# Storing the last group of an output pair by pair and moving the last subtraction from GpSimd to VectorE

## The chip, the cores and the metric

The kernel runs on one core of a Trainium2 chip. The metric is the device time of one execution in microseconds. Engines are named as in the profile: PE is TensorE (PEld its weight loads), DVE VectorE, ACT ScalarE, POOL GpSimd, SP SyncE. A "q" behind an engine's name means its sequencer.

## The reference

```
qn = q / (norm(q, axis=1) + 1e-6);  kn likewise          # q, k, v: 4 x 6336 x 256, f32
a  = softmax(kn^T @ qn / tau)                            # 256 x 256 for each batch
x  = (v @ a) as rows, 25344 x 256
H  = max(x @ w_h, 0);   T = sigmoid(x @ w_t + b_t)
out = T * H + (1 - T) * x
```

## The kernel before

A batch has 49 full slices of 128 rows and one of 64. They are worked on in 25 pairs per batch, 100 in all. For each pair PE makes z, h and x in PSUM, ACT the sigmoid tt, DVE two products th and ux, and POOL their difference. Four pairs share one output tile and go out as one store of 1 MB (1024 KB). The last pair of a batch is irregular: 128 rows and 64 rows, so two pieces and two stores. All loads but that of b_t (1 KB, by SP) cast f32 to f16 and are issued by POOL: 20 each for q and k, 12 for v, 3 for the remainders, 2 for the weights, 57 in all by the profile's list of DMA issues.

```python
    def store(t, ot):
        b, i = divmod(t, NPAIR)              # NPAIR = 25, OG = 4
        ob = out[b * N : (b + 1) * N]
        if i == NPAIR - 1:
            nc.sync.dma_start(out=rows(ob)[:, NS - 1 : NS, :], in_=ot[:, 0:1, :])
            nc.sync.dma_start(out=ob[NF:N, :], in_=ot[0:REM, 1, :])
        elif i % OG == OG - 1:
            s0 = 2 * (i - OG + 1)
            nc.sync.dma_start(out=rows(ob)[:, s0 : s0 + 2 * OG, :], in_=ot)

    def elementwise_ops(t, z, h, x, ps):
        ...                                  # tt = sigmoid(z); th = max(h,0)*tt; ux = (tt-1)*x
        ot, o0 = out_tile(t)
        for pr, us in parts:                 # one part; two in the last pair of a batch
            nc.gpsimd.tensor_tensor(
                out=ot[pr, o0 + us.start : o0 + us.stop, :], in0=th[pr, us, :],
                in1=ux[pr, us, :], op=AluOp.subtract,
            )
        store(t, ot)
```

## Time and profile before

| | before |
|---|---|
| time, median of the first 3 runs | 298.07 us (297.93 to 298.23) |
| span of the profiled run | 294.71 us |
| PE's last matmul ends | 287.13 us |
| POOL's last operation ends | 289.17 us |
| SP has seen the last store land and is through | 292.85 us |
| POOL's closing drain ends | 293.92 us |

At the end of the kernel every engine drains and meets the others at a barrier. The prediction below shows the lines. (It has 293.95 for the lowest row, from a start that its view rounds to 288.1; the trace has 288.06 + 5.86 = 293.92.)

One line is added that it doesn't show. It is from the list of PE's instructions at the end (start, duration, line, operation), and the end of that group, 287.13, is the zero: **tail** means from the end of PE's last matmul to the end of the span, here 294.71 - 287.13 = 7.58 us.

```profile
286.40 0.73 PE L366 MATMUL x<-mr,vts 128*128 128x256 f16 x4
```

The second line added is the page's group for PE's first matmul of the attention phase. Its last field is PE's idle time before it, 14.3 us, spent waiting for loads of k.

```profile
L185 PE MATMUL S<-q,k 128*128 128x256 f16 x392 | 88.0, 278 | 14.3 <-DMA k<-in_k_dram 14.3
```

### The profile page before, as it was taken

Reading aid. Unit: us, or ns where it says so; the run is one execution under the profiler, and the core shown is the slowest. Engines: PE = TensorE matmul, PEld = TensorE weight load, DVE = VectorE, ACT = ScalarE, POOL = GpSimd, SP = SyncE. Lnnn points to the kernel's source line nnn. Section 1 sums busy time; section 2 is a strip of 40 time slices with the busy share of each in tenths; the row PEclk is TensorE's granted clock in tenths of the full one; section 3 lists DMA queues with packets and bytes.
Section 4 is the critical chain, followed back from the end, with each engine's and each line's share of the span. In section 5 each row is a group of like instructions: output and inputs, shape, how many; then the busy total and the mean of one; then the engine's idle time right before and its main releaser. Section 6 shows DMA issues by size and latency. Waiting matters only on the chain.

```text
span 294.7 us, 6910 instructions
## 1 busy us (share of the span) xinstructions
PE 262.0 (89%) x2844; PEld 228.7 (78%) x2844; DVE 169.5 (58%) x318; ACT 163.5 (55%) x302; POOL 166.4 (56%) x175
## 2 busy tenths in 40 slices
PE   0497966999999999999999899999999888999990
PEld 0386944899999987899999786999998655999970
DVE  1000022675655585666666756556658777999990
ACT  1000035864453588565555596545557976989860
POOL 7111340596555775466665945455457545888882
PEclk9999988999999999999999999999999979999997
DMA  6999999999999999999999999999996631245434
GB/s 116 214 212 213 203 214 221 211 215 287 281 252 243 285 233 268 266 240 284 254 259 269 280 258 244 275 232 276 255 278 161 199 145 64 107 197 211 169 142 169
DMA packets 13233, 65.58 MB, mean 223 GB/s; under 512 B 1425, under 2 KB 3474, under 8 KB 8594
## 3 DMA queue, kind: packets, MB, share of 16 engines
q0 software_dynamic: 8848, 39.19, 65.8%
q1 hardware_dynamic: 4354, 25.96, 21.9%
q8 instruction: 22, 0.36, 0.4%
q14 instruction: 9, 0.07, 0.1%
HBM read 78.38 MB, written 25.95 MB: 354 GB/s over the span
## 4 chain that ended last, share of the span: by engine, by line
PE 72%; DMA 9%; ACT 6%; POOL 5%; DVE 4%; issue 2%; POOLq 0%; DVEq 0%
PE zbank L366 13%; PE x L366 13%; PE h L366 13%; PE S L185 11%; DMA k<-in_k_dram 9%; PE vtps L343 7%; PE G L188 6%; PE G L191 6%; POOL o L419 2%; DVE th L408 1%; PE ah L286 1%; DVE ux L413 1%; ACT tt L396 1%; ACT dcat L225 1%; PE cq L233 1%
## 5 line engine op out<-in xcount | busy, mean ns | idle before, releaser
L419 POOL TENSOR_TENSOR o<-th,ux 128x512 f32<-128x512 f32 x96 | 124.2, 1296 | 92.6 <-DVE ux L413 78.8
L366 PEld LDWEIGHTS <-vts 128*128 128x128 f16 x1200 | 109.7, 98 | 19.3 <-issue 7.9
L185 PE MATMUL S<-q,k 128*128 128x256 f16 x392 | 88.0, 278 | 14.3 <-DMA k<-in_k_dram 14.3
L396 ACT ACTIVATE tt<-zbank 128x512 f32<-128x512 f32 x100 | 59.6, 596 | 67.6 <-PE zbank L366 66.7
L408 DVE SCALAR_TENSOR_TENSOR th<-h,tt 128x512 f32<-128x512 f32 (+1 forms) x104 | 68.9, 666 | 48.6 <-PE h L366 28.4
L188 PE MATMUL G<-k 128*128 128x128 f16 x392 | 77.0, 223 | 0.0
L413 DVE SCALAR_TENSOR_TENSOR ux<-tt,x 128x512 f32<-128x512 f32 (+1 forms) x104 | 67.9, 656 | 0.7 <-PE x L366 0.7
L366 PE MATMUL x<-mr,vts 128*128 128x256 f16 (+1 forms) x400 | 61.1, 275 | 3.4 <-DVE th L408 3.4
L366 PE MATMUL zbank<-mr,vts 128*128 128x256 f16 (+1 forms) x400 | 61.0, 275 | 0.0
L366 PE MATMUL h<-mr,vts 128*128 128x256 f16 (+1 forms) x400 | 61.0, 274 | 0.0
L400 ACT COPY zbank<-btb 128x512 f32<-128x512 f32 x98 | 58.7, 599 | 1.7
L191 PE MATMUL G<-q 128*128 128x128 f16 x392 | 54.9, 222 | 0.0
L185 PEld LDWEIGHTS <-k 128*128 128x128 f16 x392 | 39.0, 100 | 18.6 <-DMA k<-in_k_dram 15.0
L358 DVE CAST vts<-vtps 128x512 f16<-128x512 f32 x50 | 34.3, 687 | 20.3 <-PE vtps L343 20.3
L188 PEld LDWEIGHTS <-k 128*128 128x128 f16 x392 | 39.1, 100 | 1.1 <-issue 0.3
L343 PE MATMUL vtps<-ident,v 128*128 128x128 f16 x392 | 38.4, 220 | 1.6 <-DVE vts L358 1.2
L343 PEld LDWEIGHTS <-v 128*128 128x128 f16 x392 | 30.0, 98 | 5.2 <-issue 2.8
L191 PEld LDWEIGHTS <-q 128*128 128x128 f16 x392 | 30.8, 100 | 2.6
L358 ACT CAST vts<-vtps 128x512 f16<-128x512 f32 x46 | 26.7, 580 | 2.3 <-PE vtps L343 2.3
L209 DVE SCALAR_TENSOR_TENSOR junk<-G,ident 128x128 f32<-128x128 f32 x16 | 3.7, 287 | 36.3 <-PE G L191 36.3
L486 ACT COPY btb<-btp 128x256 f32<-128x256 f32 x2 | 0.6, 375 | 37.5 <-PE btp L483 37.5
L107 POOL DMA_DIRECT2D k<-in_k_dram x20 | 11.3, 566 | 5.6 <-DMA k<-in_k_dram 5.3
(58 smaller groups left out, 98.2 us busy)
## 6 DMA issues: line engine op xcount, KB each, us to landing
out_dram<-o SPq DMA_DIRECT2D x24, 1024.0 KB, 10.3
q<-in_q_dram POOLq DMA_DIRECT2D x12, 768.0 KB, 22.4
k<-in_k_dram POOLq DMA_DIRECT2D x12, 768.0 KB, 24.1
v<-in_v_dram POOLq DMA_DIRECT2D x8, 1024.0 KB, 26.0
v<-in_v_dram POOLq DMA_DIRECT2D x4, 1088.0 KB, 26.0
q<-in_q_dram POOLq DMA_DIRECT2D x4, 576.0 KB, 24.6
k<-in_k_dram POOLq DMA_DIRECT2D x4, 576.0 KB, 25.0
q<-in_q_dram POOLq DMA_DIRECT2D x4, 256.0 KB, 28.0
```

Of the source, the lines that this page charges most:

```text
L107: nc.gpsimd.dma_start(out=k_t[n][:, 0:ns, :], in_=rows(k[b])[:, s0 : s0 + ns, :])
L185: nc.tensor.matmul(S[:, c, :], kc, qq[0:nr, :], start=first and c == 0, stop=last and c == 1)
L188: nc.tensor.matmul(G[:, c, :], kc, kc, start=first and c == 0, stop=False)
L191: nc.tensor.matmul(G[:, 2 + c, :], qc, qc, start=False, stop=last and c == 1)
L343: nc.tensor.matmul(ps[:, u, c, 0 : nr[u]], vt[0 : nr[u], bass.ts(c, P)], ident[0 : nr[u], 0 : nr[u]], start=(u == 0 and c == 0), stop=(u = ...
L358: cp(out=sb, in_=ps)
L366: nc.tensor.matmul(dst[0:r, u, :], sb[:, u, kt, 0:r], mr[:, kt, off : off + C], start=(not seeded and kt == 0 and (u == 0 or i == NPAIR - 1)),
L396: nc.scalar.activation(out=tt, in_=z, func=Act.Sigmoid)
L400: nc.scalar.copy(out=z, in_=btb)
L408: nc.vector.scalar_tensor_tensor(out=th[pr, us, :], in0=h[pr, us, :], scalar=0.0, in1=tt[pr, us, :], op0=AluOp.max, op1=AluOp.mult,)
L413: nc.vector.scalar_tensor_tensor(out=ux[pr, us, :], in0=tt[pr, us, :], scalar=1.0, in1=x[pr, us, :], op0=AluOp.subtract, op1=AluOp.mult,)
L419: nc.gpsimd.tensor_tensor(out=ot[pr, o0 + us.start : o0 + us.stop, :], in0=th[pr, us, :], in1=ux[pr, us, :], op=AluOp.subtract,)
```

## The change

The stores of four pairs, 20 to 23 of the last batch, and the subtraction of the last pair change. The intent is to shorten the tail of the kernel: what remains to be stored after the last pair should be small, and the last subtraction should not stand in POOL's line.

```diff
         if i == NPAIR - 1:
             nc.sync.dma_start(out=rows(ob)[:, NS - 1 : NS, :], in_=ot[:, 0:1, :])
             nc.sync.dma_start(out=ob[NF:N, :], in_=ot[0:REM, 1, :])
+        elif b == B - 1 and i >= NPAIR - 1 - OG:
+            o0 = 2 * (i % OG)
+            nc.sync.dma_start(
+                out=rows(ob)[:, 2 * i : 2 * i + 2, :], in_=ot[:, o0 : o0 + 2, :]
+            )
         elif i % OG == OG - 1:
@@
         ot, o0 = out_tile(t)
+        sub = nc.vector if t == NSLOT - 1 else nc.gpsimd
         for pr, us in parts:
-            nc.gpsimd.tensor_tensor(
+            sub.tensor_tensor(
```

## The prediction

> **What bounds the kernel now.** I began at the page to see whether the change touches the part that is long. The page's first lines:
>
> ```profile
> span 294.7 us, 6910 instructions
> PE 262.0 (89%) x2844; PEld 228.7 (78%) x2844; DVE 169.5 (58%) x318; ACT 163.5 (55%) x302; POOL 166.4 (56%) x175
> ```
>
> PE (TensorE) is busy for 262.0 of 294.7 us, and from 255 us on the chain of waits is PE without a gap. The change acts on the stores of the last five pairs only. So what can be gained lies between PE's last matmuls and the end of the span. I therefore asked for the chain that ended last in the stretch 284 to 295 us (start, duration, what):
>
> ```profile
> 283.95 0.45 PE zbank L366 x4
> 284.40 0.01 issue
> 284.40 0.69 DVE ux L413
> 285.09 0.07 issue
> 285.16 1.30 POOL o L419
> 286.46 0.01 POOLq L419
> 286.48 1.28 POOL o L419
> 287.76 0.00 issue
> 287.76 0.73 POOL ol L419
> 288.49 0.68 POOLq L583
> ```
>
> See that POOL (GpSimd) is the late engine: it runs the subtractions of pairs 22, 23 and 24 back to back. The list of POOL's instructions gives the last one as two pieces of 1.41 us together from 287.76, so POOL ends at 289.17. DVE (VectorE), by the same list for DVE, had the inputs of pair 24 ready at 287.28 + 0.73 = 288.01. Chain and engine list both stop there, 5.5 us before the span ends at 294.7. What fills these 5.5 us is stores and the closing barrier. First the issues on the SP queue (start, us, queue, line):
>
> ```profile
> 282.07 6.05 SPq L391 DMA_DIRECT2D out_dram<-o  x2
> 288.52 0.33 SPq L387 DMA_DIRECT2D out_dram<-ol  x1
> 289.20 0.96 SPq L388 DMA_DIRECT2D out_dram<-ol  x1
> ```
>
> The first line merges two stores of 1 MB; its second one starts 0.33 us before 288.12, at 287.79, so right when POOL finishes pair 23. Busy time in stretches of half a microsecond shows the DMA engines after it (last two columns: DMA share, GB/s):
>
> ```profile
> 288.00:288.50 0.50, 0.00 (x0) 0.00 (x0) 0.01 (x1) 0.00 (x0) 0.50 (x2) 1.00 0.00 0
> 288.50:289.00 0.50, 0.00 (x0) 0.00 (x0) 0.00 (x0) 0.00 (x0) 0.50 (x1) 1.00 1.03 426
> 291.50:292.00 0.50, 0.00 (x0) 0.00 (x0) 0.00 (x0) 0.00 (x0) 0.00 (x0) 0.66 0.65 172
> 292.00:292.50 0.50, 0.00 (x0) 0.00 (x0) 0.00 (x0) 0.00 (x0) 0.00 (x0) 0.50 0.00 0
> ```
>
> The first packet moves some 0.7 us after the issue, and all engines are then busy until shortly before 292. That is 1024 + 128 + 64 KB = 1.25 MB at about 400 GB/s, 3.1 us, so the two small stores stand in line behind the 1 MB. Last the end of the kernel: the instructions of the closing line (count: ns min/median/max, first and last start in us), and what SP waited for there (us in total, times, longest):
>
> ```profile
> L583 SPq EVENT_SEMAPHORE  x11: 17/28/28, 290.2 to 294.6; - x11
> L583 POOLq DRAIN  x3: 45/102/5863, 288.1 to 294.4; - x3
> L583 SPq DRAIN  x3: 7/7/7, 292.8 to 294.2; - x3
> ...
> SPq L583 <- DMA out_dram<-ol: 2.0, 1, 2.0
> SPq L583 <- PEq L583: 1.8, 2, 1.3
> ```
>
> These lines are the ones to read twice. SP waits 2.0 us from 290.2 for the last store, which has thus landed at about 292.3, checks the other semaphores and is through at 292.85. But then it waits a further 1.3 us at the barrier. POOL's drain began at 288.1 and took 5.86 us, so it ended at 293.95, later than SP by 1.1 us. PE is named as releaser, but its drain started at 285.9 and took 1.3 us. So two paths run side by side to the barrier: stores, through at 292.85, and POOL's drain, through at 293.95. POOL's is the one that binds. The rest of the barrier, 294.71 - 293.95 = 0.76 us, follows either way.
>
> **What the Trainium skill says.** "VectorE: DVE Perf Modes", section "The TRN2 errata — SBUF-src ops pay a fixed extra latency per instruction", gives an fp32 tensor_tensor of N elements (N+151)/0.96 ns, so 424 ns for 256. The trace agrees: a DVE tensor_tensor of 128x512 took 682 ns (formula 691), two-input operations of 128x256 took 402 to 424 ns. "GPSIMD Engine Reference", section "3.1 Elementwise — side-by-side cycle accounting", gives about 2.6 cycles per element; the trace has 1296 ns for 512 and 736 ns for 256 elements, so 2.19 ns per element, which at the 1.2 GHz that the same skill states is 2.6 cycles. "SBUF — State Buffer", section "SBUF: two separate sides", says that a DVE operation with two SBUF inputs and a GpSimd operation that reads SBUF lock each other out. The new DVE subtraction is of that kind; no run here shows such a pair, and it would start at 288.01, after POOL's end at 287.76. "DMA: Bandwidth & Descriptors", section "Anatomy of one DMA — SWDGE (gpsimd) path", puts a fixed 2.0 us on every DMA; of the stores here (another issue path) the quickest 128 KB landed 2.6 us after issue, so a fixed part of that order is seen.
>
> **The change, part by part.**
>
> Subtraction on DVE. It removes two POOL operations (1.41 us by the list, 287.76 to 289.17) and adds two DVE ones. DVE is free at 288.01. By the spacing of the two pieces of ux (0.73 us for two that overlap) I take 0.75 us for the pair: first piece done at about 288.42, second at 288.76. The store of the first piece can go at 288.46 instead of 288.52, that of the second at about 288.82 instead of 289.20: 0.4 us on the store path. POOL's last operation is now pair 23's, which ends at 287.76: 1.41 us earlier. The drain began in the kernel before when the last POOL operation was released by DVE (288.01, drain 288.1). With pair 23 last, which is released at 286.39 and stands behind pair 22 until 286.46, the drain begins at about 286.5, 1.6 us earlier. If what it takes is fixed, counted from its start (5.86 us), it ends at 292.35; counted from the end of the last POOL operation (293.95 - 289.17 = 4.78 us), at 292.54.
>
> Stores pair by pair. It replaces one issue of 1024 KB at 287.79 by four of 256 KB, at about 283.4, 285.1, 286.5 and 287.8 (the ends of POOL's four operations). The 1 MB of the group before, issued at 282.07, keeps the DMA engines busy until about 285.3, so pair 20's data go then; at 400 GB/s each takes 0.65 us, and pairs 20 to 22 are out by 288. Three more issues of 0.33 us fall in SP's idle time, except that pair 23's ends at 288.12, still before the first piece of pair 24 is ready. After 287.8 there remain 256 + 128 + 64 KB, 1.15 us of traffic from 288.5, done before the last piece is even moving. So the last store is no longer bound by traffic but by its issue: 288.82, plus some 0.5 us in which SP builds it (its other three took 0.47 to 0.56; the 0.96 of the last came with 1.1 MB queued), some 0.4 us to data, 0.2 us for 64 KB, 0.35 us to the semaphore: landed at about 290.3, 2.0 us sooner. SP is through 0.55 us later, at 290.85.
>
> Sum. The barrier is reached at the later of 290.85 (stores) and 292.35 to 292.54 (POOL). The end moves from 293.95 to about 292.45, by 1.5 us. The stores' gain of 2.0 us is covered by POOL's drain, of whose 1.5 us the DVE part alone is the source. Everything before 283 us is the same program. 298.07 - 1.5 = 296.57 us, 0.5% less.
>
> **The rivals.** (1) POOL's drain isn't of fixed length but ends about 1.1 us after the last store or after SP's own drain. For it: the two ends do stand 1.1 us apart. Against: the drain carries no wait on a semaphore in the trace, and POOL's own loads were over long before. Then the store path counts in full, 2.0 us: 296.1 us. (2) The drain is bound to something that doesn't move, or the removed POOL work only shows up as a longer drain: nothing gained, 298.1 us. I know of only one such drain, so I can't exclude it. (3) The small stores cost more than they save: seven issues in the tail instead of four, 2 KB runs per partition in place of 8 KB. The 128 KB store with 1 KB runs still moved at the pace of the rest, and SP is idle for 5.7 us before 287.8, so I expect nothing, but 0.3 us of late issue would be hidden beneath the drain anyhow. (4) DVE becomes the bound: it would need over a microsecond of delay at 288; it has nothing after.
>
> **Range and chances.** The three sizes of gain are 1.5 us (most likely), 2.0 us and 0. Runs of before spread over 0.3 us, and the profiled run was 1.35 us quicker than the median, so runs of another day may sit off by some tenths of a per cent. I give 296.6 us with 295.7 to 297.7. A gain over 2% would be 6 us, more than the whole tail after the last POOL operation; a loss over 2% has no source. Faster 0.01, same 0.98, slower 0.01.
>
> **What would show it.** In the profile of the changed kernel: POOL's last operation ends near 287.8 and its drain starts near 286.5, still of 5.7 to 6.0 us (right) or cut so as to end 1.1 us after SP's (rival 1) or stretched to 293.9 (rival 2); two DVE subtractions of some 0.4 us from 288.0; the last store issued near 288.8 and landed near 290.3; SP's wait at the barrier grows from 1.3 to some 1.6 to 1.8 us; span near 293.2 us. The prediction is wrong if the span falls by less than 1 us or by over 2.

## The result, and the profile after

The changed kernel took 295.77 us (median of 6 runs, 295.49 to 296.59), the kernel before 297.69 us over its 6 runs. The ratio is 0.9946, with a 95% interval of 0.9922 to 0.9969: 1.6 us faster, with 0.9 to 2.3 us in the interval. A run counts as slow when it is over 1.5% above the fastest of the same kernel. A ratio here is the mean time of one kernel's fast runs over that of the other's of the same rounds, so it isn't quite the ratio of the quoted medians.

The spans of the two traces differ by 0.6 us only, 294.71 against 294.09. The reason is not in the tail. First the page's first line and its group for PE's first matmul:

```profile
span 294.1 us, 6917 instructions
...
L185 PE MATMUL S<-q,k 128*128 128x256 f16 x392 | 87.9, 278 | 15.1 <-DMA k<-in_k_dram 15.0
```

PE waited 0.7 us longer for loads of k than in the trace of before, in a part in which the two programs are the same, and PE's last matmul ends 0.61 us later, as its list shows (287.01 + 0.73 = 287.74):

```profile
287.01 0.73 PE L366 MATMUL x<-mr,vts 128*128 128x256 f16 x4
```

The tail is 294.09 - 287.74 = 6.35 us, so 1.23 us of the 7.58 us are gone. That is less than the 1.6 us of the ratio, but within its interval. In what follows, times called "after PE" are counted from that point.

POOL's and SP's lists at the end answer to the chain and the issues of before:

```profile
284.35 4.03 POOL L425 TENSOR_TENSOR o<-th,ux 128x512 f32<-128x512 f32 x3 [0.38 <-DVE ux L418]
```

```profile
284.00 4.74 SPq L391 DMA_DIRECT2D out_dram<-o  x4
288.99 0.33 SPq L387 DMA_DIRECT2D out_dram<-ol  x1
289.41 0.47 SPq L388 DMA_DIRECT2D out_dram<-ol  x1
```

POOL ends with pair 23 at 288.38. Four small stores go between 284.00 and 288.74, and the last store is issued 1.67 us after PE (2.07 before). It took SP 0.47 us to issue instead of 0.96.

The chain that ended last looks different now, and has to be read with care:

```profile
285.68 2.20 DMA out_dram<-o
287.87 0.01 issue
287.89 0.73 DVE ux L418 x2
288.62 0.34 DVE ol L425
288.96 0.34 DVEq L589
```

It ends with DVE, as intended, but says that a store released DVE at 287.87. That is a coincidence of two semaphore events. DVE's ux starts 0.15 us after PE's last matmul in both traces (287.28 - 287.13 and 287.89 - 287.74), so what it waits for is PE. A store that held DVE would have widened that gap.

Last the closing line's instructions and SP's waits there:

```profile
L589 SPq EVENT_SEMAPHORE  x12: 17/28/28, 289.9 to 294.0; - x12
L589 POOLq DRAIN  x3: 45/102/6078, 287.0 to 293.6; - x3
L589 SPq DRAIN  x3: 7/7/114, 291.7 to 293.8; - x3
```

```profile
SPq L589 <- PEq L589: 1.8, 2, 1.6
SPq L589 <- DMA out_dram<-ol: 0.8, 2, 0.5
```

POOL's drain starts at 287.05 and takes 6.08 us, to 293.12, which is 4.75 us after POOL's last operation. Before it was 293.92 - 289.17 = 4.75 us as well. SP is through with the stores at 291.72 (3.98 us after PE; 5.72 before) and then waits 1.6 us at the barrier. The stores gained 1.74 us, POOL's drain 1.41 us (6.79 to 5.38 us after PE), and the end 1.23 us.

### The profile page after: what moved, and what is told of

It reads as the page before. It is cut to its first block, busy times and chain, and to the rows that moved or that the text cites. A ratio compares the mean times of both kernels' runs of the same rounds, so it can differ in the third digit from the quotient of the medians.

```text
span 294.1 us, 6917 instructions
## 1 busy us (share of the span) xinstructions
PE 261.9 (89%) x2844; PEld 228.6 (78%) x2844; DVE 170.3 (58%) x320; ACT 163.5 (56%) x302; POOL 165.1 (56%) x173
## 3 DMA queue, kind: packets, MB, share of 16 engines
q0 software_dynamic: 8848, 39.19, 65.8%
## 4 chain that ended last, share of the span: by engine, by line
PE 50%; DMA 20%; DVE 12%; issue 6%; ACT 5%; POOL 4%; DVEq 0%; POOLq 0%
DMA k<-in_k_dram 19%; PE S L185 10%; PE zbank L366 8%; PE h L366 8%; PE x L366 8%; DVE ux L418 6%; PE G L191 5%; PE G L188 5%; DVE th L413 4%; PE vtps L343 4%; POOL o L425 2%; DVE vts L358 1%; PE ah L286 1%; ACT tt L401 1%; ACT dcat L225 1%
## 5 line engine op out<-in xcount | busy, mean ns | idle before, releaser
L101 POOL DMA_DIRECT2D q<-in_q_dram x20 | 11.4, 571 | 5.6 <-DMA q<-in_q_dram 4.4
```

The costliest lines, as they stand in the source:

```text
L101: nc.gpsimd.dma_start(out=q_t[n][:, 0:ns, :], in_=rows(q[b])[:, s0 : s0 + ns, :])
```

## The experiments

**The theory:** the end of the kernel is bound by POOL's drain, which ends 4.75 us after POOL's last operation. **The rivals:** the stores bind it; or the drain follows the stores or SP, so that it is no cause. A second question came up on the way: where the 4.75 us are from. The profiled run of c2 was slow. All gave correct results but b2 to b4.

| run | tail us | SP through, after PE | POOL's drain ends, after PE | median us, before | ratio, 95% interval |
|---|---|---|---|---|---|
| before | 7.58 | 5.72 | 6.79 | | |
| the change | 6.35 | 3.98 | 5.38 | 295.77, 297.69 | 0.9946 (0.9922 to 0.9969) |
| a1_split_only | 7.56 | 4.37 | 6.78 | 296.99, 297.63 | 0.9980 (0.9955 to 1.0005) |
| a2_dve_only | 6.49 | 5.72 | 5.37 | 296.59, 297.63 | 0.9968 (0.9936 to 1.0000) |
| a3_two_pairs_dve | 5.36 | 4.40 | 4.07 | 294.65, 297.63 | 0.9906 (0.9876 to 0.9935) |
| a4_late_pool | 7.31 | 3.99 | 6.35 | 296.60, 297.63 | 0.9969 (0.9941 to 0.9998) |
| b1_last_group_dve | 5.91 | 4.97 | -1.61 | 297.19, 297.73 | 0.9984 (0.9950 to 1.0018) |
| c1_drain_once | 4.94 | 3.98 | 0.70 | 294.25, 297.06 | 0.9906 (0.9886 to 0.9926) |
| c2_drain_often | 4.93 | 3.98 | 0.70 | 362.22, 297.06 | 1.2150 (1.2101 to 1.2200) |
| d1_drain_before | 6.49 | 5.73 | 2.09 | 296.55, 297.06 | 0.9975 (0.9956 to 0.9994) |
| d2_drain_split | 5.14 | 4.37 | 2.10 | 294.30, 297.06 | 0.9910 (0.9891 to 0.9928) |

In every row the tail is the later of the two middle columns plus 0.76 to 0.96 us of barrier. Each row is one trace. What an edit leaves alone repeats closely: whole-group stores with SP through at 5.72, 5.72 and 5.73 us, the stores of the changed kernel at 3.98, 3.99, 3.98 and 3.98 us. So differences of 0.2 us in these columns are read as real.

### a1: the split stores alone

```diff
-        sub = nc.vector if t == NSLOT - 1 else nc.gpsimd
+        sub = nc.gpsimd
```

> The stores pair by pair, the last subtraction back on POOL. Tail = from the end of PE's last matmul to the end of the span: 7.58 us in the kernel before (294.71 - 287.13), 6.34 us in the changed one (294.08 - 287.74). Theory (POOL's drain ends a fixed 4.75 us after POOL's last operation and binds the end): POOL ends as late as before, so tail 7.5 to 7.7 us, time within 0.2 us of before, though the last store lands about 1.5 us sooner and SP then waits some 2.5 to 3 us at the barrier. Rival (the stores bind the end): tail 6.2 to 6.6 us, about 1.3 us faster.

The tail is 7.56 us, within 0.02 us of before. The last store landed 3.98 us after PE instead of 5.14, and all of this went into SP's wait for the other engines (us in total, times, longest):

```profile
SPq L589 <- PEq L589: 3.1, 2, 2.6
```

The longest wait grew from 1.3 to 2.6 us. The stores do not bind the kernel before; the rival that says so falls. The times agree, with no difference clear of noise.

### a2: the subtraction on DVE alone

```diff
-        elif b == B - 1 and i >= NPAIR - 1 - OG:
-            o0 = 2 * (i % OG)
-            nc.sync.dma_start(
-                out=rows(ob)[:, 2 * i : 2 * i + 2, :], in_=ot[:, o0 : o0 + 2, :]
-            )
```

> The last subtraction on DVE, the last group stored whole as before. Theory: POOL's drain now ends 4.75 us after pair 23, and the 1 MB store with the two small ones behind it is through about 5 us after pair 23, so the stores bind by a little: tail 6.4 to 6.7 us, 0.9 to 1.2 us faster than before, SP's wait at the barrier down to about 0. Rival (the stores bind in the kernel before already): tail 7.3 to 7.6 us, less than 0.3 us faster.

The tail is 6.49 us, 1.09 us of gain. POOL's drain was done at 5.37 us after PE and SP with the whole-group store at 5.72, so now the stores bind. SP's waits at the closing line:

```profile
SPq L584 <- DMA out_dram<-ol: 2.2, 1, 2.2
SPq L584 <- PEq L584: 0.7, 2, 0.5
```

SP's two barrier waits sum to 0.7 us, of which the longer, 0.5 us, is the second round of the barrier; at the first round, where it waited 1.3 us before, only 0.2 us are left. The two parts together gave 1.23 us. Alone they gave 0.02 and 1.09, so almost all of the gain needs the subtraction on DVE, and the stores only have to get out of its way.

### a3: pairs 23 and 24 on DVE

```diff
-        sub = nc.vector if t == NSLOT - 1 else nc.gpsimd
+        sub = nc.vector if t >= NSLOT - 2 else nc.gpsimd
```

> Changed kernel with the subtraction of pair 23 on DVE too. Theory: POOL ends with pair 22, 1.3 us sooner, so its drain does; DVE gets 0.6 us more before pair 24, of which 0.2 us falls in its idle time, so the stores go 0.4 to 0.5 us later and become the bound: tail about 5.4 us (5.2 to 5.7), 0.7 to 1.1 us faster than the changed kernel. Rival (the drain is tied to the stores or to SP, ending 1.1 to 1.4 us after SP): tail 6.7 us, slower than the changed kernel by 0.4 us.

The tail is 5.36 us. POOL's drain moved forward with POOL's last operation (0.67 us before PE's end, drain done 4.75 us later), DVE's extra operation delayed the last store by 0.42 us, and the stores bind again. A drain tied to the stores would have ended later than in the changed kernel; that rival falls. The ratio to the kernel before is 0.9906, below that of the change.

### a4: a tiny operation on POOL at the very end

```diff
         store(t, ot)
+        if t == NSLOT - 1:
+            late = work_pool.tile([P, 4], f32, tag="late", bufs=1, name="late")
+            nc.gpsimd.tensor_copy(out=late, in_=ot[:, 0, 0:4])
```

> Changed kernel with one tiny copy of 4 columns on POOL after the last subtraction on DVE, read by nobody; stores unchanged. Theory: POOL's last operation ends at about 289.45 instead of 288.38, its drain 4.75 us later, so tail 7.3 to 7.5 us, 1.0 to 1.2 us slower than the changed kernel and about as slow as the kernel before, with the stores landing as early as in the changed kernel. Rival (stores bind, or the drain follows SP): tail 6.2 to 6.5 us, no difference to the changed kernel.

Stores and DVE are as in the changed kernel to within 0.01 us. POOL's list and its drain:

```profile
289.00 0.32 POOL L432 COPY late<-ol 128x4 f32<-128x4 f32 x1 [0.67 <-DVE ol L425]
```

```profile
L592 POOLq DRAIN  x3: 45/93/5088, 289.0 to 294.6; - x3
```

A copy of 0.32 us that nobody reads moved the end by 0.96 us: the drain is over at 294.06, again 4.75 us after POOL's last operation, and the tail is 7.31 us. The drain is a cause. The times point the same way (0.9969 against 0.9946) but would not have settled it.

### b1: no subtraction of the last five pairs on POOL

```diff
-        sub = nc.vector if t == NSLOT - 1 else nc.gpsimd
+        sub = nc.vector if t >= NSLOT - 5 else nc.gpsimd
```

> Changed kernel with the subtractions of all five last pairs (20 to 24) on DVE, so POOL ends with pair 19, some 5.7 us before its end in the changed kernel. Theory (drain 4.75 us from POOL's last operation, in all five traces so far): the drain is over before SP is through, SP's wait at the barrier is about 0.03 us, and the stores alone bind. DVE gets 0.6 us more in each of pairs 20 to 23 where PE needs 1.3 us a pair, so it becomes the bound there and the stores go 1 to 2 us later than in the run with two pairs on DVE: 0.5 to 1.8 us slower than that run. Rival (the drain's end has a floor set by SP's or DVE's end): drain still ends about 0.5 us or more after DVE's last operation plus 2 us, and its length from POOL's last operation is over 8 us.

The closing line's drains on POOL, and SP's waits at that line:

```profile
L589 POOLq DRAIN  x3: 45/102/6083, 282.2 to 295.4; - x3
```

```profile
SPq L589 <- PEq L589: 0.4, 2, 0.2
```

The drain ran from 282.22 to 288.30, 4.75 us after POOL's last operation at 283.56 and over before PE had ended. It has no floor from other engines. SP still waits 0.2 us at the first round of the barrier (I had expected 0.03 us): this is the barrier itself. The cost to DVE was larger than I expected: 2.3 us by the ratios against a3 (0.9984 - 0.9906 of 297.7 us), where I had said 0.5 to 1.8. DVE's th of one pair started 1.92 us after that of the pair before where PE sets 1.31 us, and PE had to wait for DVE too, so its last matmul ended at 289.92.

### b2, b3, b4: the drain by itself

The whole body was replaced (so the result is wrong): n loads of 256 KB of f32 (128 KB once cast) from POOL's queue with n = 0, 1 and 20, then four dependent subtractions of 128x512 on POOL, then one store.

```python
    for n in range(loads):
        nc.gpsimd.dma_start(out=l[:, n, :, :], in_=q[n % B, 0 : 2 * P, :].rearrange(...))
    ...                                       # DVE waits for the last load
    for n in range(4):
        nc.gpsimd.tensor_tensor(out=o, in0=a, in1=got, op=AluOp.subtract)
    nc.sync.dma_start(out=..., in_=o)
```

> Not the kernel but the disputed cost by itself (wrong result on purpose): four POOL subtractions of 128x512 and one store, no load from POOL's queue. If the 4.75 us after POOL's last operation belong to the DMAs that POOL issued, the drain is short here (under 0.3 us after the last operation, as the 0.19 us drain at the start of the kernel before). If it is a property of ending POOL's work, it is 4.75 us here too.

> The same with one load of 256 KB issued by POOL ahead of the subtractions. DMAs as the cause, fixed cost: 4.75 us. DMAs as the cause, cost per DMA: about 0.1 us (4.75 us over the 51 loads of the kernel). Property of POOL's end: 4.75 us, as without a load.

> The same with 20 loads of 256 KB issued by POOL. Fixed cost of having used DMAs, or property of POOL's end: 4.75 us. Cost per DMA: about 1.9 us. None of the theories of the end of the kernel hangs on this; it tells what a writer could change to shorten the drain.

The closing line's drains of the three runs, in this order:

```profile
L95 POOLq DRAIN  x3: 34/73/1362, 5.9 to 9.8; - x3
```

```profile
L95 POOLq DRAIN  x3: 34/83/1453, 9.3 to 13.2; - x3
```

```profile
L95 POOLq DRAIN  x3: 34/96/3012, 23.3 to 27.3; - x3
```

The longest is the first drain. It starts while the last subtraction, 1.26 us long, is still to run, so from its end we take off the end of that operation: 7.28 - 7.22 = 0.06 us without a load, 10.73 - 10.57 = 0.16 us with one, 26.35 - 24.64 = 1.71 us with 20. The prediction by cost per load had said 0.1 and 1.9 us. From 0 to 20 loads it is (1.71 - 0.06) / 20 = 0.083 us each; from 0 to the kernel's 57 it is (4.75 - 0.06) / 57 = 0.082 us each. (The second expectation divides by 51 loads; the list of issues has 57.) POOL's drain grows with the number of DMAs that POOL has issued. It does not go by bytes: POOL's queue moved 2.62 MB in the run with 20 loads and 39.19 MB in the kernel, 15 times as much for 2.8 times the drain. It could go by packets, since a load is 144 packets there and 155 on average in the kernel; the count of loads fits better (0.083 and 0.082 us a load, 0.57 and 0.53 ns a packet), but no run separates the two. What the drain does for each load no run shows.

### c1 and c2: a drain earlier

```diff
         run(t, "post")
+        if t == 70:                          # c1
+            nc.gpsimd.drain()
```

```diff
         run(t, "post")
+        if t <= 72 and t % 4 == 0:           # c2
+            nc.gpsimd.drain()
```

> Changed kernel with one more drain on POOL at pair 70 of 100, after the last load has been issued. The three runs of the drain by itself gave 0.06, 0.16 and 1.71 us after POOL's last operation for 0, 1 and 20 loads from POOL's queue, so 0.08 us per load; 57 loads make 4.75 us. If a drain clears what the loads before it left, the early one takes about 4.7 us in the middle, which POOL makes up (1.30 us a pair against 1.53) before the end, and the last drain ends within 0.2 us of POOL's last operation: the stores bind, SP's wait at the barrier is about 0.03 us, tail 4.8 to 5.0 us, 1.3 to 1.5 us faster than the changed kernel. If every drain pays for all loads so far: last drain again 4.75 us, tail 6.35 us, time as the changed kernel or slower. If the delay of 4.7 us isn't made up: PE's last matmul comes later.

> Changed kernel with a drain on POOL at every fourth pair up to pair 72. If a drain clears what came before: 19 drains of 0.1 to 0.7 us after the operation before each (the first about 2 us, for some 25 loads), POOL hardly late anywhere, tail 4.8 to 5.0 us, and at least as fast as the run with one drain. If a drain among loads in flight waits until they land, some of these drains take 10 us and more, POOL's subtractions stop, and the kernel is slower than the changed one by several us. If every drain pays for all loads so far: 19 drains of 2 to 4.7 us, about 65 us in all on POOL, 20 us and more slower.

In c1 the early drain, the closing drains and SP's wait at the barrier are:

```profile
L542 POOLq DRAIN  x1: 6075/6075/6075, 240.2 to 240.2; - x1
```

```profile
L591 POOLq DRAIN  x3: 39/102/1399, 287.5 to 292.7; - x3
```

```profile
SPq L591 <- PEq L591: 0.4, 2, 0.2
```

The early drain pays the 4.75 us after its operation (241.56 to 246.30), while the other engines go on: PE is busy for 5.8 of the 6.4 us from 240.0, as in the changed kernel in the same work. The last packet of a load had moved at 232.65, so this drain waited for none; and it took as long as the closing one though only 81 of POOL's 110 arithmetic operations lay behind it, so it does not go by these either. POOL's last operation comes 0.64 us after PE's end, exactly as in the changed kernel, so the delay was made up. The closing drain ends 0.07 us after it. A drain clears what came before it. The tail is 4.94 us and the stores alone bind.

c2 shows the limit. The same instruction among loads in flight, by the list of its line:

```profile
L542 POOLq DRAIN  x19: 1412/11711/26145, 55.2 to 314.2; - x19
```

The median of the 19 drains is 11.7 us and the longest 26.1 us, POOL cannot issue the next loads meanwhile, and the kernel takes 362.22 us, by its fast runs 21.5% longer. Of what I had named, a drain that waits for loads in flight fits, and the packed trace shows it: 16 of the 19 drains end 0.3 to 1.3 us after the last packet of the loads in flight has moved, and the other three, with none in flight, end 0.08 us after the POOL operation queued before them. A cost for all loads so far doesn't fit, as c2's closing drain ends 0.07 us after POOL's last operation.

### d1 and d2: what the change is worth without the drain

The early drain of c1 was put into the kernel before (d1) and into a1 (d2).

> The kernel before, with nothing of the change, and the early drain at pair 70. POOL's last drain then ends right after its last operation, 2.1 us after PE's last matmul, and what binds is the 1 MB store with the two small ones behind it: SP through 5.72 us after PE's last matmul as in the kernel before, tail 6.4 to 6.6 us, 1.0 to 1.2 us faster than before. It would be as fast as the changed kernel (tail 6.35 us) without any of the change. If the tail stays at 7.5 us, the drain wasn't what bound the kernel before.

> The stores pair by pair, the last subtraction on POOL, and the early drain. The gain that the split stores had behind POOL's drain should come to light: SP was through 4.37 us after PE's last matmul in the run with the split alone, so tail 5.1 to 5.4 us, 1.1 to 1.4 us faster than the run with the early drain and whole stores. Against the run with the whole change and the early drain (tail 4.94 us) it should lack 0.2 to 0.4 us: that is all that the subtraction on DVE is worth once the drain is out of the way.

In d1 the longest drain of the closing line is now 1.17 us, 288.96 to 290.13, and ends 0.07 us after POOL's last operation:

```profile
L585 POOLq DRAIN  x3: 39/102/1171, 289.0 to 294.3; - x3
```

With the drain out of the way the tail is 6.49 us for the kernel before, 5.14 us with the split stores, 4.94 us with both parts. The order of worth is turned round: the split stores, worth 0.02 us in a1, are worth 1.35 us here, and the subtraction on DVE, worth 1.09 us in a2, is worth 0.20 us. Neither kernel changed in these parts; what changed is which path ends last. By the times d1 is 0.7 us faster than before (0.2 to 1.3 us in the interval, where I had expected 1.0 to 1.2), d2 2.7 us.

c1, d2 and a3 come out below both given kernels, with ratios of 0.9906, 0.9910 and 0.9906 to the kernel before against 0.9946 of the changed one. Their intervals just touch or overlap that of the changed kernel, so the clearer witness are the tails: 4.94, 5.14 and 5.36 us against 6.35. The times don't separate the three; c1 has the shortest tail.

## Why the prediction was right or wrong

It was right in the mechanism and in the gain (1.5 us; 1.6 us by the ratio, 1.23 us in the tails). The time itself (296.6 us with 295.7 to 297.7; measured 295.77) was met with some luck: it lies 0.07 us inside the range, in part because the 298.07 us it was counted from, the median of three runs, became 297.69 us over six. And one of its own signs of being wrong came true: the span fell by 0.62 us, not by the 1 to 2 us that it had named. The span was a poor test, as PE's longer wait for loads of k (0.7 us in that one trace, in unchanged code) hid half of the 1.23 us. By its steps:

- **POOL's drain binds, not the stores.** Right, and shown by a1 and a4, not only read from one wait of SP.
- **The drain takes a fixed time from POOL's last operation.** Right: of the two countings offered, 4.78 us from the last operation's end holds (4.74 or 4.75 us unrounded in every trace without an early drain), 5.86 us from the drain's start doesn't (5.09 to 6.08 us). It was a guess then; b2 to b4 and c1 tie the constant to POOL's 57 loads. Rival 1 (drain follows stores or SP) fell with a1, where the drain ended 2.41 us after SP was through instead of 1.1, and with a3 and b1, rival 2 (nothing moves) with the result.
- **DVE takes over in 0.75 us from when ux is ready.** Right: 0.75 us, in overlapping pieces of 409 and 411 ns.
- **Last store issued 1.69 us after PE** (288.82 - 287.13): 1.67 us. **Landed 3.17 us after PE:** wrong in size, 3.59 us. I had summed 0.5 + 0.4 + 0.2 + 0.35 us from issue to landing; the store took 1.92 us. In the packed trace the same terms are 0.47 us of SP, 0.65 us to the first packet, 0.45 us of packets and 0.34 us to the last semaphore event, so the second and third were too small. It was hidden behind the drain, as were the stores' other gains.
- **The rest of the barrier follows either way with 0.76 us.** Wrong by 0.2 us. From the drain's end to the end of the span it took 0.96 us: SP began its drain of the second round 0.5 us after it was released there, and took 0.114 us for it instead of 0.007. All runs that have both the split stores and a subtraction on DVE show this, none of the others does. Its cause is open. It explains why the drain gained 1.41 us and the end 1.23.
- **"The DVE part alone is the source" of the gain.** Nearly: alone it gives 1.09 us, and then the whole-group store binds.
- **Rivals 3 and 4** (cost of small stores, DVE as bound): no sign of either in the changed kernel; b1 shows where DVE does become the bound, and in a3 it delays the stores, which bind there.

One thing was left out altogether: that POOL's drain, once recognised as the bound, could be made short for itself. The best kernels here come from that, or from ending POOL's work earlier.

The lock between a DVE operation with two SBUF inputs and a POOL operation, which the prediction mentions, stays untested: in the changed kernel DVE's subtractions began at 288.55, after POOL's end at 288.38. In a4 the tiny POOL copy (289.00 to 289.31) did run beside DVE's second piece (288.85 to 289.26). DVE took its usual 409 ns; whether the copy waited for it can't be told, since no run has the copy alone.

## What to carry to other kernels

At the end of a kernel several paths run side by side to the barrier; look at each engine's closing drain and at who waits there before shortening any of them, since the chain of compute instructions stops short of them. If POOL has issued many DMAs, its last operation should come early, or a drain should be placed after the last load has landed and well before the end, where POOL can make up the time; among loads in flight it does harm. A gain that vanishes behind another path is not lost: measure it again when that path is gone.

## What the Trainium skill lacked or had wrong

- POOL's closing drain and its cost per DMA issued from POOL: 0.06, 0.16, 1.71 and 4.75 us after POOL's last operation for 0, 1, 20 and 57 DMAs. No page has it; that it goes by loads and not by packets is likely and not shown; it would belong in "GPSIMD Engine Reference".
- A drain on POOL while its loads are in flight: a median of 11.7 us and up to 26.1 us. No page has it.
- "VectorE: DVE Perf Modes", section "The DRAIN you can't avoid", tells the drains after DVE operations from those of the preamble and postamble, said to be about 12 ns on all five engines. It has no place for a third kind that is seen here: closing drains that carry a line of the kernel's own file and last as long as 5.86 us on POOL, 1.32 us on PE, 0.88 us on DVE and 0.007 us on SP in the kernel before.
- "DMA: Bandwidth & Descriptors", section "Anatomy of one DMA — SWDGE (gpsimd) path", gives 2.0 us plus the bytes at 436 GB/s for POOL's path, which makes an estimate of 2.15 us for 64 KB. The page has no such sum for transfers that SP issues; here the last stores of the changed kernel took 1.9 us for 64 KB and 1.8 us for 128 KB.
